# Moving the transposes of queries and keys from TensorE to the DMA crossbar in a fused attention and feed-forward kernel

## The chip, the cores and the metric

The kernel runs on one core of a Trainium2 chip. The metric is the time of one execution in device microseconds; lower is better. A median of several runs is quoted with its range. Ratios are computed as the mean time of one kernel's fast runs over the mean time of the other's fast runs of the same rounds, so they are not quite the ratios of the medians quoted beside them.

In the text, a "chunk" is 512 tokens of the feed-forward part. There are nine chunks and eight batches of attention.

## The reference, cut to what matters

```python
def _attn_ref(q, k, v, global_idx):          # q, k, v: (8 batches, 8 heads, 576, 64) fp32
    scores = q @ k.T / sqrt(64)              # band of +-32 positions, 8 global positions
    attn = softmax(where(mask, scores, -1e9))
    return attn @ v

def reference(...):
    x = attn_out as (4608 tokens, 512)
    g, val = x @ w_gate, x @ w_val           # 512 x 1536 each
    return (silu(g) * val) @ w_out           # 1536 x 512
```

## The kernel before

The score matmuls of both kernels take queries and keys with the head dimension on partitions, the rows of on-chip memory (`qT`, `kT`). They arrive in DRAM with tokens as rows. The kernel before loads them with a cast to bf16 during the DMA and transposes them on TensorE, in four groups (`step_T`) per batch:

```python
def step_T(hp):                                   # four of these a batch
    for name in ("k", "q"):
        ps = pm.tile([P, LJ, LP], BF16, tag="m", name="ps_t")
        for j in range(LJ):
            for par in range(2):
                nc.tensor.transpose(out=ps[64 * par : 64 * par + 64, j, :],
                    in_=ld[name][:, 2 * hp + par, D * j : D * (j + 1)], ...)
        if name == "k":  nc.scalar.copy(out=kT[...], in_=ps...)
        else:            nc.vector.tensor_copy(out=st["qT"][...], in_=ps...)
```

Attention of the next batch is cut into 16 steps, one after each of the 16 feed-forward steps of a chunk (12 "gates" and 4 output steps), so that TensorE has matmuls while ScalarE and VectorE work:

```python
return [
    [L(step_T, 0), L(step_GT)], [L(step_T, 1)], [L(step_T, 2), vb], [L(step_T, 3)],
    [L(step_S2)], [L(step_SG)], [L(step_P2T), L(step_S, 0)], [L(step_S, 1), L(step_AV2)],
    # ... cut: scores (S), attention times values (AV), output transposes (X)
]
```

`vb` is a copy of the values, shifted by 64 tokens, that two DMAs on SyncE's queue make from SBUF to SBUF. `step_GT` transposes the gathered global queries and keys (`kqm`). The scheduling is manual, so every engine issues its work in this order:

```python
loaded[0] = new_qk(); load_qk_part(0, ...)        # GpSimd's queue, casting
g0 = gather(0); load_v(0); kqms[0] = gather_mask(*g0)
for i in range(3): load_wgv(i)                    # 6 weight loads, 1 MB of fp32 each
prefetch(1)                                       # batch 1: gather, q, k, v
# ... cut: output weights wo
for s in attention(0): ...                        # batch 0, nothing to overlap it with
for c in range(NCH):                              # 9 chunks
    for i, f in enumerate(ffn(c)):
        f()                                       # gate or output step
        # then step i of attention(c + 1)
        if i == 2 and c + 2 < B: prefetch(c + 2)
```

The softmax here doesn't subtract the row's maximum and nothing guards it: scores larger than these inputs give would overflow.

## Time and profile before

The median is 428.41 us (428.28 to 428.94, three runs).

| what | value | where read |
|---|---|---|
| span | 426.4 us | the page |
| TensorE busy | 389.9 us | the page |
| first gate of the feed-forward part | 44.0 us | timeline of TensorE |
| length of a steady chunk | 44.9 us | distance of the same step in two chunks |

In the views PE is TensorE, PEld its weight loads, DVE VectorE, ACT ScalarE, POOL GpSimd, and SP or SPq SyncE and its queue. The following lines are from the page of the kernel before. The first gives busy microseconds, the share of the span and number of instructions by engine. The next three give 40 equal slices of the span in tenths: TensorE busy, TensorE clock granted, DMA engines busy. The last gives the shares of the chain that ended last.

```profile
PE 389.9 (91%) x3786; PEld 191.7 (45%) x3786; DVE 265.9 (62%) x583; ACT 178.9 (42%) x281; POOL 92.8 (22%) x134
...
PE   0467899999999999999999999999999999999996
...
PEclk9999999999999999999999999999999999999999
DMA  7999999874338363738355735500030002002002
...
PE 77%; DVE 13%; ACT 5%; POOL 2%; issue 2%; DVEq 0%; ACTq 0%; POOLq 0%
```

TensorE has work from the fourth slice on and almost never stops. The chain is 77% TensorE, so time taken from TensorE in the chunks is time taken from the kernel. The DMA engines are nearly full in the first seven slices (to about 75 us) and then have room.

The stage table of the kernel before (busy microseconds of each engine in a stretch, then clock, DMA share and rate; the share adds up the times of all packets and can pass 1) has the start and one chunk:

```profile
core 0: us, PE busy (x) PEld busy (x) DVE busy (x) ACT busy (x) POOL busy (x), PEclk, DMA share, GB/s
...
15.00:44.00 29.00, 18.67 (x288) 12.26 (x289) 13.95 (x41) 10.88 (x15) 16.59 (x23) 1.00 1.31 184
...
91.00:135.90 44.90, 43.55 (x457) 21.36 (x455) 29.82 (x66) 20.93 (x34) 9.79 (x14) 1.00 0.51 78
```

In the chunk TensorE works 43.55 of 44.9 us. From 15 to 44 us, when batch 0's attention runs alone, it works only 18.67 of 29 us.

The timeline of TensorE before (start, microseconds, engine, line, instruction) shows the first gate and, in a later chunk, one gate with a transpose group:

```profile
43.97 1.91 PE L523 MATMUL pg<-xT,wg_sb 128*128 128x512 bf16 x4
...
138.86 1.02 PE L523 MATMUL pg<-xT,wg_sb 128*128 128x512 bf16 x4
139.72 1.03 PE L523 MATMUL pv<-xT,wv_sb 128*128 128x512 bf16 x4
140.68 0.45 PE L282 MATMUL ps_t<-ident,k_bf 96*64 96x96 bf16 x12
140.96 0.42 PE L282 MATMUL ps_t<-ident,q_bf 96*64 96x96 bf16 x12
141.31 1.04 PE L523 MATMUL pg<-xT,wg_sb 128*128 128x512 bf16 x4
```

From gate to gate it is 141.31 − 138.86 = 2.45 us. The matmuls of the gate alone take two times 0.86 us in the ordered chain, so a transpose group costs about 0.73 us.

The timeline of SyncE's queue before shows the first of batch 0's two `vb` copies:

```profile
20.18 0.53 SPq L100 DMA_DIRECT2D vb<-va  x1
```

They are issued at 20 to 21 us, in good time for their first use at 31 us. On GpSimd's timeline before, the last weight load is issued at 22 us, and a value load that waits for that weight load to land runs at 41 us:

```profile
22.05 0.79 POOL L212 DMA_DIRECT2D wv_sb<-in_moe_w_val_dram  x1
...
41.04 3.42 POOL L95 DMA_DIRECT2D va<-in_v_dram  x4 [1.81 <-DMA wv_sb<-in_moe_w_val_dram]
```

So what stands several transfers behind the weights on GpSimd's queue begins at about 40 us.

### The profile page before, as it was taken

Reading aid. Unit: us, or ns where it says so; the run is one execution under the profiler, and the core shown is the slowest. Engines: PE = TensorE matmul, PEld = TensorE weight load, DVE = VectorE, ACT = ScalarE, POOL = GpSimd, SP = SyncE. Lnnn points to the kernel's source line nnn. Section 1 sums busy time; section 2 is a strip of 40 time slices with the busy share of each in tenths; the row PEclk is TensorE's granted clock in tenths of the full one; section 3 lists DMA queues with packets and bytes.
Section 4 is the critical chain, followed back from the end, with each engine's and each line's share of the span. In section 5 each row is a group of like instructions: output and inputs, shape, how many; then the busy total and the mean of one; then the engine's idle time right before and its main releaser. Section 6 shows DMA issues by size and latency. Waiting matters only on the chain.

```text
span 426.4 us, 9039 instructions
## 1 busy us (share of the span) xinstructions
PE 389.9 (91%) x3786; PEld 191.7 (45%) x3786; DVE 265.9 (62%) x583; ACT 178.9 (42%) x281; POOL 92.8 (22%) x134
## 2 busy tenths in 40 slices
PE   0467899999999999999999999999999999999996
PEld 0344444444544444454444444444444444444442
DVE  5456488638871888278835794488628871771760
ACT  1153355345633464256524653356245643323321
POOL 8943847132023201412122211100000000000000
PEclk9999999999999999999999999999999999999999
DMA  7999999874338363738355735500030002002002
GB/s 111 71 204 208 187 223 154 91 151 57 58 31 131 67 99 22 109 84 113 23 74 117 112 22 73 116 0 3 25 121 7 2 2 94 6 0 98 2 0 98
DMA packets 62232, 33.74 MB, mean 79 GB/s; under 512 B 39408, under 2 KB 56304, under 8 KB 62192
## 3 DMA queue, kind: packets, MB, share of 16 engines
q0 software_dynamic: 55584, 19.40, 40.3%
q1 hardware_dynamic: 6608, 13.77, 9.8%
q8 instruction: 29, 0.48, 0.5%
q14 instruction: 11, 0.09, 0.1%
HBM read 38.28 MB, written 9.44 MB: 112 GB/s over the span
## 4 chain that ended last, share of the span: by engine, by line
PE 77%; DVE 13%; ACT 5%; POOL 2%; issue 2%; DVEq 0%; ACTq 0%; POOLq 0%
PE po L539 22%; PE pg L523 19%; PE pv L523 18%; PE ps_t L282 4%; PE ps_av L435 4%; DVE pt L401 4%; PE ps_av L426 3%; ACT pe L396 3%; DVE h L534 2%; DVE xa L414 2%; PE ps_x L466 2%; ACT kT L288 1%; PE ps_s L388 1%; DVE gvt L365 1%; DVE gv L531 1%
## 5 line engine op out<-in xcount | busy, mean ns | idle before, releaser
L531 DVE SCALAR_TENSOR_TENSOR gv<-th,pg 128x512 bf16<-128x512 bf16 x108 | 73.9, 685 | 62.1 <-ACT th L529 62.1
L523 PE MATMUL pg<-xT,wg_sb 128*128 128x512 bf16 x432 | 112.5, 383 | 0.0
L523 PE MATMUL pv<-xT,wv_sb 128*128 128x512 bf16 x432 | 111.8, 381 | 0.0
L539 PE MATMUL po<-wo_sb,h 128*128 128x512 bf16 x432 | 98.4, 380 | 0.0
L529 ACT ACTIVATE th<-pg 128x512 bf16<-128x512 f32 x108 | 64.5, 598 | 69.1 <-PE pg L523 67.9
L534 DVE TENSOR_TENSOR h<-gv,pv 128x512 bf16<-128x512 bf16 x108 | 74.2, 687 | 11.9 <-PE ps_s L388 0.5
L523 PEld LDWEIGHTS <-wv_sb 128*128 128x128 bf16 x432 | 42.5, 98 | 51.6 <-issue 1.1
L95 POOL DMA_DIRECT2D va<-in_v_dram x40 | 33.8, 853 | 124.7 <-PE ps_av L435 92.5
L539 PEld LDWEIGHTS <-h 128*128 128x128 bf16 x432 | 40.2, 98 | 45.3
L544 ACT ACTIVATE osb<-po 128x512 f32<-128x512 f32 x36 | 21.5, 597 | 92.7 <-PE po L539 92.7
L523 PEld LDWEIGHTS <-wg_sb 128*128 128x128 bf16 x432 | 36.1, 98 | 38.2 <-issue 4.1
L396 ACT ACTIVATE pe<-ps_s 128x1024 bf16<-128x1024 f32 (+1 forms) x40 | 37.6, 940 | 14.8 <-PE ps_s L388 14.8
L410 DVE TENSOR_REDUCE den<-ps_av 128x4 f32<-128x8 f32 x72 | 11.4, 158 | 44.4 <-PE ps_av L455 36.0
L288 ACT COPY kT<-ps_t 128x576 bf16<-128x576 bf16 x32 | 20.4, 638 | 37.4 <-PE ps_t L282 37.4
L401 DVE TENSOR_TENSOR pt<-pe,band 128x1024 bf16<-128x1024 bf16 (+1 forms) x40 | 25.4, 634 | 11.1 <-ACT pe L396 11.0
L414 DVE TENSOR_TENSOR xa<-ps_av,den 128x256 bf16<-128x256 f32 x72 | 30.5, 424 | 2.5
L293 DVE COPY qT<-ps_t 128x576 bf16<-128x576 bf16 x32 | 24.0, 749 | 2.8 <-PE ps_t L282 2.8
L472 ACT COPY xT<-ps_x 128x512 bf16<-128x512 bf16 x32 | 18.0, 588 | 13.8 <-PE ps_x L466 13.8
L426 PE MATMUL ps_av<-gvt,pg 128*128 128x264 bf16 x64 | 19.0, 297 | 3.5 <-DVE gvt L373 2.8
L435 PE MATMUL ps_av<-va,pt 128*64 128x66 bf16 x256 | 21.0, 206 | 0.0
L435 PE MATMUL ps_av<-vb,pt 128*64 128x66 bf16 x256 | 21.0, 207 | 0.0
L435 PEld LDWEIGHTS <-pt 128*64 128x64 bf16 x512 | 13.9, 114 | 14.7 <-issue 10.4
(93 smaller groups left out, 271.1 us busy)
## 6 DMA issues: line engine op xcount, KB each, us to landing
out_dram<-osb SPq DMA_DIRECT2D x36, 256.0 KB, 2.0
k_bf<-in_k_dram POOLq DMA_DIRECT2D x16, 288.0 KB, 6.4
q_bf<-in_q_dram POOLq DMA_DIRECT2D x16, 288.0 KB, 7.2
vb<-va SPq DMA_DIRECT2D x16, 264.0 KB, 3.8
va<-in_v_dram POOLq DMA_DIRECT2D x24, 128.0 KB, 4.0
va<-in_v_dram POOLq DMA_DIRECT2D x16, 96.0 KB, 3.6
wg_sb<-in_moe_w_gate_dram POOLq DMA_DIRECT2D x3, 512.0 KB, 13.2
wv_sb<-in_moe_w_val_dram POOLq DMA_DIRECT2D x3, 512.0 KB, 15.0
```

The source lines that it names most:

```text
L95: nc.gpsimd.dma_start(out=va[lo:hi, u, :, 0:D], in_=vs[t0 + lo : t0 + hi])
L288: nc.scalar.copy(out=kT[:, hp, WIN : WIN + S].rearrange("p (i j) -> p i j", j=LJ), in_=ps.rearrange("p j i -> p i j"),)
L396: nc.scalar.activation(out=pe, in_=ps[:, :, 0 : 64 * ns].rearrange("p r (s c) -> p r s c", c=64), func=AF.Exp, scale=SCALE,)
L401: nc.vector.tensor_tensor(out=pt.rearrange("p r s c -> p (r s) c"), in0=pe.rearrange("p r s c -> p (r s) c"), in1=bc(band, [[0, 2 * ns], [ ...
L414: nc.vector.tensor_tensor(out=xa, in0=ps[:, :, 0:D], in1=den.to_broadcast([P, 4, D]), op=ALU.mult)
L426: nc.tensor.matmul(out=ps, lhsT=st["pg"][:, P * tp : P * (tp + 1)], rhs=st["gv"].rearrange("p h r c -> p (h r) c")[:, 4 * hg : 4 * hg + 4, :],
L435: nc.tensor.matmul(out=ps[64 * e : 64 * e + 64, hl, :], lhsT=pt[:, hl % 2, slot, :], rhs=vv[:, tp, 4 * hg + hl, :], start=False, stop=(hl ...
L523: nc.tensor.matmul(out=ps, lhsT=w[:, cc, P * fc : P * (fc + 1)], rhs=xT[:, cc, t0 : t0 + CH], start=(cc == 0), stop=(cc == NCC - 1),)
L529: nc.scalar.activation(out=th, in_=pg, func=AF.Tanh, scale=0.5)
L531: nc.vector.scalar_tensor_tensor(out=gv, in0=th, scalar=1.0, in1=pg, op0=ALU.add, op1=ALU.mult)
L534: nc.vector.tensor_tensor(out=st["h"][:, fc, :], in0=gv, in1=pv, op=ALU.mult)
L539: nc.tensor.matmul(out=po, lhsT=st["h"][:, fc, P * ts : P * (ts + 1)], rhs=wo_sb[:, fc, :], start=(fc == 0), stop=(fc == NFC - 1),)
```

## The change

From batch 1 on, TensorE no longer transposes. A DMA casts queries and keys to a bf16 scratch in DRAM in token order. A crossbar transpose, a DMA on SyncE's queue, brings them to SBUF as `kT` and `qT`. Values come uncast on SyncE's queue and are cast by GpSimd. The intent is to take 96 transposes and eight copies a batch off TensorE, ScalarE and VectorE. The core of the diff:

```diff
+    def cast_qk(b):
+        for name, src in (("k", k), ("q", q)):
+            t = dram.tile([S, H, D], BF16, name=f"{name}f{b}")
+            nc.gpsimd.dma_start(out=t, in_=src[b].rearrange("h s d -> s h d"))
+            flat[name, b] = t
+    def transpose_qk(b):
+        kT = kT_bufs[b % 2]
+        nc.sync.dma_start_transpose(out=kT[:, :, WIN : WIN + S], in_=flat["k", b]...)
+        qT = bp.tile([P, HP, S], BF16, tag="qT", name="qT")
+        nc.sync.dma_start_transpose(out=qT, in_=flat["q", b]...)
...  (load_v_raw: five loads on nc.sync; cast_v: six nc.gpsimd.tensor_copy)
+        if b > 0:
+            head = [[got, L(step_GT)], [vb]]          # 2 steps instead of 4
...
-    prefetch(1)
+    cast_qk(1)
+    cast_qk(2)
+    kqms[1] = gather_mask(*gather(1))
     for i in range(4):                                # output weights
...
+    cast_v(1, load_v_raw(1))
+    transpose_qk(1)
     for s in attention(0):
...
-            if i == 2 and c + 2 < B:
-                prefetch(c + 2)
+            if i == 1 and c + 2 < B:
+                transpose_qk(c + 2)
+                if c + 3 < B:
+                    cast_qk(c + 3)
+                kqms[c + 2] = gather_mask(*gather(c + 2))
+                vsts[c + 2] = load_v_raw(c + 2)
+            if i == 6 and c + 2 < B:
+                cast_v(c + 2, vsts[c + 2])
```

More of the change, by code (lines that the diff above doesn't have):

```diff
@@ L61 @@
     wpool = ctx.enter_context(tc.tile_pool(name="wpool", bufs=1))
-    ldp = ctx.enter_context(tc.tile_pool(name="ldp", bufs=2))
+    ldp = ctx.enter_context(tc.tile_pool(name="ldp", bufs=1))
+    dram = ctx.enter_context(tc.tile_pool(name="dram", bufs=1, space=bass.MemoryType.DRAM))
     bp = ctx.enter_context(tc.tile_pool(name="bp", bufs=2))
@@ L95, in load_v, with load_v_raw, cast_v @@
             nc.gpsimd.dma_start(out=va[lo:hi, u, :, 0:D], in_=vs[t0 + lo : t0 + hi])
+    def load_v_raw(b):
+        vst = ldp.tile([P, 5, H, D], FP32, tag="vst", name="vst")
+        vs = v[b].rearrange("h s d -> s h d")
+        for u in range(5):
+            lo = WIN if u == 0 else 0
+            hi = P - WIN if u == 4 else P
+            t0 = P * u - WIN
+            nc.sync.dma_start(out=vst[lo:hi, u], in_=vs[t0 + lo : t0 + hi])
+        return vst
+    def cast_v(b, vst):
+        va = va_bufs[b % 2]
+        nc.gpsimd.tensor_copy(out=va[WIN:64, 0, :, 0:D], in_=vst[WIN:64, 0])
+        nc.gpsimd.tensor_copy(out=va[64:P, 0, :, 0:D], in_=vst[64:P, 0])
+        for u in range(1, 4):
+            nc.gpsimd.tensor_copy(out=va[:, u, :, 0:D], in_=vst[:, u])
+        nc.gpsimd.tensor_copy(out=va[0 : P - WIN, 4, :, 0:D], in_=vst[0 : P - WIN, 4])
+    flat = {}
+    def cast_qk(b):
[3 more added lines that the diff above has]
+            flat[name, b] = t
+    tr = {}
+    def transpose_qk(b):
+        kT = kT_bufs[b % 2]
+        nc.sync.dma_start_transpose(
+            out=kT[:, :, WIN : WIN + S], in_=flat["k", b].rearrange("s h d -> s (h d)")
+        )
+        qT = bp.tile([P, HP, S], BF16, tag="qT", name="qT")
+        nc.sync.dma_start_transpose(
+            out=qT, in_=flat["q", b].rearrange("s h d -> s (h d)")
+        )
+        tr[b] = qT
     def load_vb(b):
@@ L268, in attention @@
     def attention(b):
-        ld = loaded[b]
+        ld = loaded[0] if b == 0 else None
         kT = kT_bufs[b % 2]
@@ L489, in vb, with got @@
             st["vb"] = load_vb(b)
+        def got():
+            st["qT"] = tr[b]
         L = lambda f, *a: (lambda: f(*a))
-        return [
+        head = [
             [L(step_T, 0), L(step_GT)],
@@ L496, in attention @@
             [L(step_T, 3)],
+        ]
+        if b > 0:
+            head = [[got, L(step_GT)], [vb]]
+        return head + [
             [L(step_S2)],
@@ L549, in ffn @@
         return [L(gate, fc) for fc in range(NFC)] + [L(outp, ts) for ts in range(4)]
+    vsts = [None] * B
     def prefetch(b):
-        loaded[b] = new_qk()
         g = gather(b)
-        load_qk_part(b, loaded[b], 0)
-        load_qk_part(b, loaded[b], 1)
-        load_v(b)
+        cast_qk(b)
+        vsts[b] = load_v_raw(b)
         kqms[b] = gather_mask(*g)
-    prefetch(1)
+    cast_qk(1)
+    cast_qk(2)
+    kqms[1] = gather_mask(*gather(1))
     for i in range(4):
```

## The prediction

> **What bounds it now.** The page puts TensorE at 389.9 of 426.4 us, and the chain of waits is 77% TensorE. In the steady chunks (stage table, 45 us stretches from 100 to 325 us) TensorE works 43.65 of 45 us, so a chunk with a batch of attention inside is TensorE-bound. The first 44 us are not: there the chain is batch-0 attention behind its loads, and the DMA engines are full to about 75 us (page, DMA row).
>
> **Removed, for batches 1 to 7.** Per batch 96 TensorE transposes (four groups of 24), four ScalarE copies (638 ns) and four VectorE copies (750 ns). In the TensorE timeline a gate with a transpose group takes 2.46 us (138.86 to 141.31) against 1.73 us for its eight matmuls: 0.72 us each, 2.9 us a batch. The short wait of the gathered-key transpose for the ScalarE copy (0.48 us) goes too: at most 3.4 us a batch, 24 us in all. I keep 19 to 20, because attention now starts two slots earlier, which puts the last attention-value products and output transposes into gate slots, where VectorE (two 0.69 us operations a gate, 0.7 us per normalisation) is already in the chain (13% of it).
>
> **Added.** Each query or key tensor becomes a DRAM-to-DRAM cast of 4608 pieces of 128 bytes, against 768 pieces of 768 bytes. Value loads of the same piece size move at about 117 GB/s written (15 to 20 us), some 18 ns a piece per engine; with a DRAM target I estimate 18 to 30 ns, so 5 to 9 us per tensor. A crossbar transpose of 0.59 MB: the Trainium skill, "DMA: Bandwidth & Descriptors", Latency and other measured facts, gives 261 GB/s, hence an estimate of 2.3 us plus landing; no trace here shows it, and I allow up to 10. In steady chunks this has a whole chunk of slack and should hide; GpSimd (9.8 of 45 us busy) has room for the casts of values.
>
> **Where it hurts: the start.** On SyncE's program order both transposes of batch 1 come before the shifted value copy (vb) of batch 0, and they wait for both casts of batch 1. These casts stand on GpSimd's queue behind all six gate/value weight loads, whose last lands at 41 us (GpSimd's waits for them end at 31.4, 33.4, 35.9, 38.4, 41.0). So casts land near 48 and 56, the transposes land near 62, vb near 65 to 70. Before, vb was issued at 20 us and used at 31. TensorE stands in batch 0's first attention-value step from 31 to about 68, then needs its remaining 13 us; the first gate starts near 82 instead of 44. The gathers of batch 1 stand behind four casts (to about 75), which may add little more. About +40 us, all on the critical path, paid once.
>
> **Sum.** 428.4 + 40 − 19.5 = 449 us, range 432 to 480. Chances: faster by over 2% 0.05, within 2% 0.10, slower 0.85.
>
> **Signs.** Right: TensorE idle of some 35 us from about 31, released by the vb copy; first gate near 80; chunk period 42 instead of 45; transposes and casts hidden after batch 1; TensorE busy down by about 27 us. Wrong: first gate near 44 (no stall), or chunk period still 45.
>
> **What would make it wrong.** Casts of 3 us and fast transposes bring it near 435. Casts over 15 us or transposes over 12 us make DMA the bound of every chunk and the result 500 or more. If VectorE becomes the bound in gate slots, the saving shrinks below 14.

## The result and the profile after

The changed kernel took 439.69 us (438.52 to 441.35, four runs), against 428.68 us for the kernel before. The profiled run is the slowest of the four (441.35 us). The ratio is 1.0257 (95% interval 1.0219 to 1.0294): slower by 2.6%. The same lines of the page as above, for the changed kernel:

```profile
PE 367.5 (84%) x3066; PEld 177.8 (40%) x3114; DVE 247.6 (56%) x555; ACT 162.3 (37%) x253; POOL 102.3 (23%) x127
...
PE   0450026999999999899989999999999999999996
...
PEclk9999999999999999999999999999999999999999
DMA  9999999994987919492979490059013001002002
...
PE 57%; DVE 23%; DMA 6%; ACT 4%; POOL 3%; SPq 3%; issue 3%; DVEq 0%; ACTq 0%; POOLq 0%
```

TensorE is busy for 22 us less, and the span is 13 us longer in this profile. The new hole, a stand of TensorE, is in the fourth to sixth slices of the TensorE row, while the DMA row reads 9. The waits by engine (who waited for whom: total, times, longest) name it, and the second line is a stall of GpSimd that is used below:

```profile
PE ps_av L475 <- DMA vb<-va: 32.0, 1, 32.0
...
POOL qf L121 <- issue: 11.8, 1, 11.8
```

One wait of 32 us, on the shifted value copy of batch 0. The chain in order of time (start, microseconds, what) says why that copy was late:

```profile
22.95 19.94 DMA kf<-in_k_dram
...
42.91 5.67 SPq L128
...
48.63 6.91 SPq L132
...
55.73 0.54 SPq L140
...
56.32 7.23 DMA vb<-va
...
63.59 0.43 PE ps_av L475 x7
```

The key cast, issued at 23 us, lands at 42.9. Only then can SyncE issue the key transpose (L128), which occupies its queue for 5.7 us, and then the query transpose (L132), for 6.9 us. The copy that batch 0 needs is behind both, is issued at 55.7, and lands at 63.6. For batch 0 the order of issue changed only in this copy's place on SyncE's queue.

The stage table of the changed kernel, for that stand and for one later chunk (columns as before):

```profile
31.30:63.50 32.20, 0.32 (x2) 0.13 (x1) 0.50 (x1) 0.00 (x0) 4.36 (x4) 1.00 1.75 165
...
163.70:205.80 42.10, 40.36 (x353) 19.34 (x359) 27.24 (x62) 18.57 (x29) 11.38 (x12) 1.00 0.87 125
```

The later chunk takes 42.1 us instead of 44.9, and TensorE is busy in it for some 3 us less (a few matmul records are missing in this trace). So the change does two things. The first gate moves from 44.0 to 77.2 us, a loss of 33.2 us paid once (the timeline of TensorE; one record of the four matmuls is missing):

```profile
77.22 1.49 PE L570 MATMUL pg<-xT,wg_sb 128*128 128x512 bf16 x3 [0.22 <-issue]
```

From there to the end it takes 439.6 − 77.2 = 362.4 us instead of 426.4 − 44.0 = 382.4, a gain of 20.0 us. The difference is 13.2 us, which is the difference of the two profiled spans.

### The profile page after: what moved, and what is told of

Read it like the earlier page. It is cut to its first block, busy times and chain, and to the rows that moved or that the text cites. A ratio compares the mean times of both kernels' runs of the same rounds, so it can differ in the third digit from the quotient of the medians.

```text
span 439.6 us, 7623 instructions
## 1 busy us (share of the span) xinstructions
PE 367.5 (84%) x3066; PEld 177.8 (40%) x3114; DVE 247.6 (56%) x555; ACT 162.3 (37%) x253; POOL 102.3 (23%) x127
## 2 busy tenths in 40 slices
DMA packets 148466, 46.04 MB, mean 105 GB/s; under 512 B 136400, under 2 KB 142544, under 8 KB 148432
## 3 DMA queue, kind: packets, MB, share of 16 engines
q1 hardware_dynamic: 72128, 30.29, 33.1%
## 4 chain that ended last, share of the span: by engine, by line
PE 57%; DVE 23%; DMA 6%; ACT 4%; POOL 3%; SPq 3%; issue 3%; DVEq 0%; ACTq 0%; POOLq 0%
PE po L586 21%; PE pg L570 15%; PE pv L570 13%; DVE xa L454 5%; DVE h L581 5%; DMA kf<-in_k_dram 5%; DVE pt L441 4%; DVE gv L578 4%; DVE den L453 2%; ACT pe L436 2%; DMA vb<-va 2%; SPq L132 2%; PE ps_x L506 2%; PE ps_av L475 1%; SPq L128 1%
## 5 line engine op out<-in xcount | busy, mean ns | idle before, releaser
L570 PE MATMUL pg<-xT,wg_sb 128*128 128x512 bf16 x401 | 110.1, 385 | 2.9 <-issue 1.3
L586 PE MATMUL po<-wo_sb,h 128*128 128x512 bf16 x417 | 94.9, 379 | 0.5
L581 DVE TENSOR_TENSOR h<-gv,pv 128x512 bf16<-128x512 bf16 x108 | 74.3, 688 | 11.5 <-PE pv L570 0.4
L586 PEld LDWEIGHTS <-h 128*128 128x128 bf16 x432 | 41.1, 98 | 46.3
L570 PEld LDWEIGHTS <-wg_sb 128*128 128x128 bf16 x432 | 37.2, 99 | 41.1 <-issue 4.6
L441 DVE TENSOR_TENSOR pt<-pe,band 128x1024 bf16<-128x1024 bf16 (+1 forms) x40 | 26.7, 668 | 11.3 <-ACT pe L436 11.2
L110 POOL CAST va<-vst 32x512 bf16<-32x512 f32 x7 | 4.2, 603 | 120.7 <-DMA vst<-in_v_dram 73.3
L121 POOL DMA_DIRECT2D qf<-in_q_dram x7 | 18.8, 2687 | 11.8 <-issue 11.8
L475 PE MATMUL ps_av<-va,pt 128*64 128x66 bf16 x256 | 21.3, 207 | 0.0
L506 PE MATMUL ps_x<-ident,xa 128*128 128x128 bf16 x128 | 13.5, 232 | 7.5 <-DVE xa L454 7.2
## 6 DMA issues: line engine op xcount, KB each, us to landing
wg_sb<-in_moe_w_gate_dram POOLq DMA_DIRECT2D x3, 512.0 KB, 11.5
```

Source lines behind the costliest of these rows:

```text
L441: nc.vector.tensor_tensor(out=pt.rearrange("p r s c -> p (r s) c"), in0=pe.rearrange("p r s c -> p (r s) c"), in1=bc(band, [[0, 2 * ns], [ ...
L475: nc.tensor.matmul(out=ps[64 * e : 64 * e + 64, hl, :], lhsT=pt[:, hl % 2, slot, :], rhs=vv[:, tp, 4 * hg + hl, :], start=False, stop=(hl ...
L506: nc.tensor.transpose(out=ps[:, hp, :], in_=st["xa", tp][:, 2 * hp : 2 * hp + 2, :].rearrange("p h d -> p (h d)"), identity=ident,)
L570: nc.tensor.matmul(out=ps, lhsT=w[:, cc, P * fc : P * (fc + 1)], rhs=xT[:, cc, t0 : t0 + CH], start=(cc == 0), stop=(cc == NCC - 1),)
L581: nc.vector.tensor_tensor(out=st["h"][:, fc, :], in0=gv, in1=pv, op=ALU.mult)
L586: nc.tensor.matmul(out=po, lhsT=st["h"][:, fc, P * ts : P * (ts + 1)], rhs=wo_sb[:, fc, :], start=(fc == 0), stop=(fc == NFC - 1),)
```

## The experiments

My theory: the gain in the chunks is real and the DMA work is hidden there; the loss is only the order of issue at the start. Rivals: the traffic of casts and transposes slows everything (the DMA packets rise from 62,232 to 148,466); or the crossbar transposes themselves are too slow. Every edit is shown against the changed kernel unless said otherwise. Every run was judged correct against the reference. Between rounds the kernel before moved by 0.5 us.

| run | median us | ratio to before | new waits of TensorE, us (after the first gate unless said) | steady chunk us |
|---|---|---|---|---|
| before | 428.4 to 428.9 | 1 | none | 44.90 |
| changed | 439.69 | 1.0257 | 32.0 before the first gate | 42.10 |
| e1_vb_first | 426.94 | 0.9964 | 17.0 | 41.95 |
| e2_gather_first | 425.59 | 0.9925 | 11.3 + 3.3 | 42.06 |
| e3_casts_before_weights | 421.62 | 0.9835 | 12.2 | 42.16 |
| e4_free_transposes | 409.42 | 0.9552 | none | 42.28 |
| e5_late_slots | 437.33 | 1.0202 | 30.8 before the first gate | 41.85 |
| e6_casts_early_only | 434.94 | 1.0142 | 26.6 before the first gate | 42.28 |
| e7_early_casts_late_slots | 415.69 | 0.9695 | 7.9 | 41.61 |
| e8_values_as_before | 429.64 | 1.0029 | 11.5 + 3.6 + 2.1 | 41.77 |
| e9_batch1_on_tensore | 428.52 | 0.9991 | 18.1 | 41.80 |
| e10_casts_first | 426.01 | 0.9941 | 12.8 before the first gate | 41.81 |
| e11_batch1_vb_fixed | 408.65 | 0.9541 | none | 41.68 |
| e12_fixed_dma_values | 407.31 | 0.9511 | none | 41.47 |

The steady chunk is the mean distance between ScalarE's last output copies of batches 1 to 5 (before) or 1 to 6 (the others).

### e1: vb ahead of the transposes

```diff
-    transpose_qk(1)
     for s in attention(0):
         for f in s:
             f()
+    transpose_qk(1)
```

> The changed kernel with one move: the two transposes of batch 1 are put after batch 0's attention in the program, so that on SyncE the shifted value copy of batch 0 (vb) is issued first. Same DMA work, same arithmetic. My theory (order on SyncE): no 32 us stand of TensorE on vb; first gate at 44 to 46 us instead of 77; then a new wait, at the gathered-key transpose of batch 1, because the gathers still stand behind the four casts (kqm at 64 us in the changed kernel): about 18 us. Total 424 to 428 us. Rival A (the sheer DMA traffic of casts and transposes delays everything): the first gate stays beyond 70 us and the total within 4 us of 439.7. Rival B (vb itself is slow beside the casts whatever its place): stand of over 20 us remains.

Measured: 426.94 us, within its range. SyncE's queue in this run:

```profile
20.48 0.54 SPq L140 DMA_DIRECT2D vb<-va  x1
...
45.10 5.53 SPq L128 DMA_TRANSPOSE kT<-kf  x1
50.74 7.17 SPq L132 DMA_TRANSPOSE qT<-qf  x1
```

The copy is issued at 20.5 us again, the first gate is at 44.1 us, and the stand of 32 us is gone, with the same DMA work. The transposes still occupy the queue for 5.5 and 7.2 us. Both rivals fall as the explanation of that stand. The wait that was expected behind it shows in the waits of TensorE:

```profile
PE ps_g L342 <- POOL kqm L233: 22.9, 2, 17.0
```

Of these, 5.9 us is batch 0's own wait, which the kernel before has too; the other 17.0 us is the gathered keys of batch 1 behind four casts. In the changed kernel this wait was hidden by the longer one.

### e2: the gathers ahead of the casts as well

```diff
 (e1, and)
-    cast_qk(1)
-    cast_qk(2)
-    kqms[1] = gather_mask(*gather(1))
+    g1 = gather(1)
+    cast_qk(1)
+    kqms[1] = gather_mask(*g1)
     (output weights)
+    cast_qk(2)
```

> e1 plus: the gathers of batch 1 before its casts on GpSimd's queue, and the casts of batch 2 after the output weights. Theory: the new wait at the gathered keys goes; left is the wait for the batch-1 transposes themselves, which are wanted at 49 to 53 us and land at about 55 (keys) and 58 to 62 (queries): 5 to 9 us. Total 412 to 418 us. If the steady chunks, not the start, were what loses, it stays above 425.

Measured: 425.59 us, a miss. The wait for the gathered keys went, but the waits for the transposes themselves were longer than I expected:

```profile
PE ps_s L371 <- DMA kT<-kf: 11.3, 1, 11.3
...
PE ps_sg L353 <- DMA qT<-qf: 3.3, 1, 3.3
```

That is 14.6 us instead of 5 to 9. The key transpose was issued at 46.0 us and took 16.3 us to land, where 6.6 us was the shortest in the changed kernel. Beside it the output weights and the casts of batch 2 were on the DMA engines. The second rival is therefore not dead for the start: a transpose among full queues is slow.

### e3: the casts of batch 1 ahead of the weights

```diff
 (e2, and the gather and the casts of batch 1 moved up)
+    g1 = gather(1)
+    cast_qk(1)
     for i in range(3):
         load_wgv(i)
```

> e2 with the gathers and the casts of batch 1 moved ahead of the six gate/value weight loads on GpSimd's queue; vb of batch 0 before the transposes as in e1. Theory (only the order at the start lost the time): two casts cost about 7.5 us of DMA time (4608 pieces each at 158 GB/s written), so they land near 32 us, the transposes (12 to 13 us of SyncE's issue while the rings are full) land near 46, the first weights near 36: first gate at 44 to 45, no wait over 3 us, total 409 to 413 us, the free-transposes kernel being 409.4. Rival (with the DMA rings full the transposes land late wherever they stand): a wait of 5 us or more for the transposed keys stays, total above 415.

Measured: 421.62 us, a miss; the rival's total came, with the wait on the transposed queries and not the keys. SyncE's queue in this run:

```profile
29.96 6.53 SPq L128 DMA_TRANSPOSE kT<-kf  x1
36.60 19.15 SPq L132 DMA_TRANSPOSE qT<-qf  x1
```

The key cast lands by 30 us and the query cast by 34, but the query transpose then holds the queue for 19.2 us. The DMA view of e3 from 36.6 to 56 us (queue, packets, megabytes, share; then one issue and its time to landing) shows why:

```profile
q0 software_dynamic: 2897, 2.87, 93.1%
q1 hardware_dynamic: 2899, 0.73, 35.0%
...
qT<-qf SPq DMA_TRANSPOSE x1, 29.1
```

In this stretch the queue that SyncE feeds (q1) got 2899 packets through while the queue that GpSimd feeds (q0) got 2897. The Trainium skill, "DMA: Bandwidth & Descriptors", section Queues, rings and completion order, says that each DMA engine goes round-robin between the queues that have work, a packet at a time. This trace agrees: one for one. So do e6 and e10 beside weights (625 to 625 packets from 40 to 44 us, 624 to 624 from 36 to 40). Beside casts the counts are not equal (922 of SyncE's to 407 from 49 to 51 us in the changed kernel). Whether the trace's packets are those of the page is not shown. GpSimd's packets here are mostly pieces of weights (2.87 MB in 2897 packets, about 1 KB written each; the 2 KB in the expectation of e10 are the same rows as read in fp32). The transpose's packets are about 250 bytes. (The changed kernel's q1 has 72,128 packets; less 32,256 of values and 6,608 as before the change, 33,264 are left for 14 transposes, 2,376 for each of 0.59 MB.) So a transpose needs some 2,400 turns, and beside weights it pays for each with a weight packet. At the 624 packets that SyncE's queue got through from 44 to 48 us, 2,376 take an estimated 15 us. The query transpose landed 29.1 us after its issue, but behind the key transpose, which landed 20.8 us after its own: 14.9 us apart.

### e4: what free transposes would give

```diff
-        kT = kT_bufs[b % 2]
+        kT = kT_bufs[0]
...
-            st["qT"] = tr[b]
+            st["qT"] = tr[0]        # batch 0's, kept
 (all cast_qk and transpose_qk removed)
```

> Wrong result on purpose: the changed kernel with no casts of queries and keys and no crossbar transposes at all; batches 1 to 7 read batch 0's transposed keys and queries. The slot order, values and everything else as in the changed kernel. It is what the change would give if its DMA cost nothing. Theory: chunks of 42.0 us, the same as in the changed kernel, since the casts and transposes are hidden there; first gate near 44; total 406 to 409 us. Rival (DMA traffic also slows the chunks): chunks of 41 us or less, total below 402.

Measured: 409.42 us, just above its range, with a chunk of 42.28 us against 42.10 in the changed kernel. Removing all casts and transposes makes no chunk shorter, so in the chunks they cost nothing. That settles the first rival for the chunks. This kernel computes with the wrong queries and keys from batch 1 on. The comparison with the reference still passed it, presumably because queries and keys are scaled by 0.1 and the scores are all near zero. A "correct" on this input says little about `qT` and `kT`.

### e5: the old slots

```diff
-            head = [[got, L(step_GT)], [vb]]
+            head = [[got, L(step_GT)], [vb], [], []]
```

> The changed kernel with two empty steps put in where the transposes were, so that the attention of a batch stands in the same slots of the chunk as before the change. My prediction said that the two slots earlier cost some 0.5 us a chunk through VectorE. If so, the chunk falls from 42.0 to about 41.5 and the total by 3 to 4 us, to 436. Rival (the slots do not matter, TensorE is the bound either way): within 1 us of the changed kernel. Note that its prologue is unchanged, so the 33 us stay.

Measured: 437.33 us, ratio 1.0202 against 1.0257: about 2.4 us less, where 3 to 4 were expected; the traced stand is 1.2 us shorter, so not all of it is the slots. Across all runs that differ in this the chunk is 41.6 to 41.85 us with the two empty steps (e5, e7, e9, e10, e11) and 41.95 to 42.3 without (changed, e1, e2, e3, e4, e6). The two pairs that differ in this alone give 0.25 us (changed and e5) and 0.55 us (e3 and e7), the means of the two groups 0.39 us. So the earlier slots cost some 0.4 us a chunk.

### e6: only the casts moved

```diff
-    cast_qk(1)
     cast_qk(2)
...
+    cast_qk(1)
     for i in range(3):
         load_wgv(i)
```

> The changed kernel with one move only: the casts of batch 1 go ahead of the weight loads; the transposes still stand before vb on SyncE. It splits the 32 us stand of TensorE: the part that is the casts' place behind the weights (31.3 to 42.9 us in the changed kernel) should go, the part that is SyncE issuing the transposes and vb landing behind them (12.8 and 7.8 us) should stay. Theory: casts land near 32, transposes issue to about 45, vb lands near 50: a stand of 17 to 22 us, the batch-1 gathers (behind two casts of batch 2 only after the weights) no worse than before; total 425 to 430. Rival (the whole stand is the weights' place in the queue): stand under 8 us, total below 417.

Measured: 434.94 us and a stand of 26.6 us. This is longer than I expected, and for the reason found in e3. SyncE's queue:

```profile
27.89 9.07 SPq L128 DMA_TRANSPOSE kT<-kf  x1
37.01 12.32 SPq L132 DMA_TRANSPOSE qT<-qf  x1
49.58 0.55 SPq L140 DMA_DIRECT2D vb<-va  x1
```

The key cast is done 15 us earlier than in the changed kernel (27.9 against 42.9 us), but the transposes now meet the weights and hold SyncE for 9.1 and 12.3 us instead of 5.7 and 6.9. Only 5.4 us of the stand go. So moving the casts alone gains little, because the transposes then meet the weights; what is left is the place of `vb` behind two slow transposes.

### e7: e3 with the old slots

The edit is e3 and the line of e5.

> e3 with the two empty steps of e5. Theory: the start of e3 and the chunk of e5 (41.85 against 42.1 us): 1 to 3 us below e3, near 408 to 411. If the slots bring nothing, the same as e3 within 0.7 us.

Measured: 415.69 us, better than e3 by more than the slots explain. The query transposes are wanted two gates later, so the wait for them is 7.9 instead of 12.2 us. Even so the total missed its range.

### e8: e3 with the values as before

```diff
 (e3, and)
-    cast_v(1, load_v_raw(1))
+    load_v(1)
...
-                vsts[c + 2] = load_v_raw(c + 2)
-            if i == 6 and c + 2 < B:
-                cast_v(c + 2, vsts[c + 2])
+                load_v(c + 2)
```

> e3 with the value part of the change undone: values are again cast by the DMA into place, with no staging tile and no casts on GpSimd. Theory: in the chunks both hide behind TensorE, so within 2 us of e3. Rival (value part matters, because GpSimd's in-order queue stands waiting for the value buffers and so issues the next casts late): a wait for transposes appears and the total is over 3 us above e3.

Measured: 429.64 us, 8 us above e3: a miss, and the rival's total came, though by another way. The loss is all in the first chunk, where the values of batch 1 now stand behind the casts of batch 2 on GpSimd's queue (5.7 us of new waits for values and their copy; the 11.5 us for the transposed queries were 12.2 in e3). The 5.7 us are not all of it: TensorE's granted clock was 0.50 to 0.57 from 74 to 89 us, where in e3 it was 1.00. The later chunks are shorter, 41.77 against 42.16 us. The groups of VectorE by shape, from 140 to 300 us, show a reason (total busy, then mean nanoseconds of one). In the changed kernel:

```profile
L441 DVE TENSOR_TENSOR pt<-pe,band 128x1024 bf16<-128x1024 bf16 x13 | 9.6, 739 | 2.1 <-ACT pe L436 2.1
```

And the same group in e8:

```profile
L444 DVE TENSOR_TENSOR pt<-pe,band 128x1024 bf16<-128x1024 bf16 x16 | 11.0, 687 | 2.7 <-ACT pe L439 2.7
```

The band product, with two SBUF inputs, takes 739 ns where GpSimd casts values and 687 ns where it does not. The kernel before has 686 ns. The Trainium skill, "SBUF — State Buffer", section Who interferes with whom, says that a VectorE instruction with two SBUF inputs contends with a GpSimd instruction that reads SBUF. The numbers agree with that. The DMA work is not the reason: e4, with GpSimd's casts but without the DMA work of queries and keys, has 733 ns. Whether these 50 ns make the shorter chunk is not shown.

### e9: batch 1 on TensorE

```diff
-    cast_qk(1)
-    cast_qk(2)
-    kqms[1] = gather_mask(*gather(1))
+    g1 = gather(1)
+    loaded[1] = new_qk()
+    load_qk_part(1, loaded[1], 0)
+    load_qk_part(1, loaded[1], 1)
+    kqms[1] = gather_mask(*g1)
     (output weights)
+    cast_qk(2)
...
-        if b > 0:
-            head = [[got, L(step_GT)], [vb]]
+        if b > 1:
+            head = [[got, L(step_GT)], [vb], [], []]
 (transpose_qk(1) removed)
```

> Batch 1 goes the old way (plain loads, transposes on TensorE), casts and crossbar transposes start with batch 2, where nothing is in a hurry; two empty slots as in e7. Theory: no wait for a transpose anywhere; the free-transposes kernel (409.4) plus one batch of TensorE transposes (2.9 us) less the later slots (about 1.7 us): 409 to 413 us. Rival (crossbar transposes also come too late for batch 2): a wait at batch 2 and over 415.

Measured: 428.52 us, a miss, by my own edit. SyncE's queue:

```profile
58.58 6.50 SPq L128 DMA_TRANSPOSE kT<-kf  x1
65.20 6.60 SPq L132 DMA_TRANSPOSE qT<-qf  x1
71.98 8.30 SPq L105 DMA_DIRECT2D vst<-in_v_dram  x5
80.33 1.04 SPq L140 DMA_DIRECT2D vb<-va  x1
```

The old step list makes batch 1's `vb` in the third step, but the transposes of batch 2 are issued in the second. So `vb` stood behind two transposes and five value loads, and TensorE waited 18.1 us for it: the fault of the changed kernel over again, one batch later.

### e10: the casts in the early gap

```diff
     load_qk_part(0, loaded[0], 1)
+    cast_qk(1)
...
-    cast_qk(1)
-    cast_qk(2)
     kqms[1] = gather_mask(*gather(1))
     (output weights)
+    cast_qk(2)
 (and the line of e5)
```

> The casts of batch 1 directly behind batch 0's own query and key loads, where the DMA engines stood idle before (10 to 15 us); transposes before vb on SyncE as in the changed kernel; two empty slots. It tests why the query transpose took 19 us of issue in e3 and e7. Theory (the transpose shares each DMA engine packet by packet with what else is queued, and there these were 2 KB weight packets): here its neighbours are mostly 128-byte value and cast packets, so each transpose issues in 4 to 8 us, all lands by about 32, vb by about 36; TensorE waits under 6 us for it, and no wait later. Batch 0's own gathers and values land some 3 to 7 us later. Total 410 to 418. Rival (a transpose is just slow at the start, 19 us whatever stands beside it): vb beyond 42, total over 420.

Measured: 426.01 us, a miss. The transposes were issued from 20.6 us and held SyncE for 5.8 and 8.4 us, as the theory of neighbours expected; the rival's 19 us did not come. But the query transpose landed 22.3 us after its issue, `vb` after 42 us and the total over 420, as the rival had it. There were two costs I had not counted, and the waits of TensorE show both:

```profile
PE ps_i L276 <- DVE ones L273: 15.0, 1, 15.0
PE ps_av L476 <- DMA vb<-va: 12.8, 1, 12.8
```

The casts occupy GpSimd while it should write the small index tables, so VectorE's opening work, and TensorE's first wait with it, ends at 15.0 us instead of 10.4 (kernel before); batch 0's wait for its gathered keys grows from 5.8 to 8.5 us. And `vb`, issued at 35.2 to 38.6 us, took up to 14.8 us to land. The weights were then on the engines and the transposes' packets ahead of it on the same queue. How those two share the 14.8 us is not separated.

### e11: e9 with vb in its right place

```diff
 (e9, and)
-            [L(step_T, 1)],
-            [L(step_T, 2), vb],
+            [L(step_T, 1), vb],
+            [L(step_T, 2)],
```

> e9 with batch 1's vb moved one slot up, so that on SyncE it stands before the transposes of batch 2. In e9 the 18.1 us wait for vb of batch 1 came from my own edit: the old step list put vb of batch 1 in the slot after the transposes of batch 2 are issued, the very order that hurts the changed kernel. Theory: no wait over 2 us after the first gate; first chunk near 47 us, later chunks 41.8; total 409 to 412 us. Rival (something else in the start of e9 costs the 18 us): over 418.

Measured: 408.65 us (408.12 to 409.41, five runs), just below its range, ratio 0.9541. SyncE's queue:

```profile
52.64 0.46 SPq L140 DMA_DIRECT2D vb<-va  x1
...
60.51 6.07 SPq L128 DMA_TRANSPOSE kT<-kf  x1
```

`vb` of batch 1 at 52.6 us precedes the transposes of batch 2 at 60.5 us, and no new wait is left. Moving one copy by one slot was worth 20 us, more than the 18.1 us of the wait. In e9 the granted clock was still 0.50 from 84 to 89 us, when TensorE had begun to work again, and 0.66 from 89 to 94; that may be the rest.

### e12: e11 with values cast by the DMA from batch 2 on

```diff
 (e11, and)
-                vsts[c + 2] = load_v_raw(c + 2)
-            if i == 6 and c + 2 < B:
-                cast_v(c + 2, vsts[c + 2])
+                load_v(c + 2)
```

> e11 with the values of batches 2 to 7 loaded and cast by the DMA as before the change; batch 1's values stay as in e11. The band product on VectorE (128x1024) takes 739 ns in the changed kernel's chunks and 687 ns in e8, where GpSimd casts nothing; if GpSimd's casts beside VectorE cost the chunk, this is 1 to 2.5 us below e11 (chunk 41.5 instead of 41.8). If they are hidden, it equals e11 within 0.7 us. If the value loads delay the casts on the shared queue, it is above e11.

Measured: 407.31 us (406.78 to 407.62, five runs), ratio 0.9511 (0.9498 to 0.9524), the fastest and 32 us below the changed kernel. The gain over e11 is 1.3 us, as expected if GpSimd's casts cost the chunk, so the value part of the change is a small loss in the chunks; at the start, beside early casts, it was useful (e8). Two lines of its page, TensorE by slices and the shares of the chain:

```profile
PE   0367899999999999999999999999999999999996
...
PE 76%; DVE 14%; ACT 4%; POOL 2%; issue 2%; DMA 1%; DVEq 0%; ACTq 0%; POOLq 0%
```

The hole is gone and the chain is again TensorE. Against the kernel before, six batches save 44.90 − 41.47 = 3.43 us each, which is 20.6 of the 21.1 us.

## Why the prediction was right, point by point

- **Direction and mechanism were right.** The prediction named `vb` of batch 0 behind the transposes of batch 1 on SyncE, and these behind the casts behind the weights. The chain shows exactly these links, and e1 removes the stand by moving one line.
- **The gain in the chunks was right in sum, in part by luck.** I kept 19 to 20 us; the part after the first gate became 20.0 us shorter. The upper limit of 3.4 us a batch is also what e12 reaches (3.43). I had taken 0.64 us a batch off it for the slots alone; the runs show some 0.4 for the slots and 0.2 for the value part (e11 against e12), which I had not counted.
- **The loss was overestimated by some 7 us.** The prediction's 449 had +40 for this term and the runs show +33. (The other part of the distance to 439.7 is mostly that the profiled run is the slowest of the four.) Two terms were mis-sized and cancelled, which was luck. The casts were estimated at 5 to 9 us a tensor; while only casts ran, the DMA wrote 158 GB/s, so 0.59 MB takes 3.7 us, and the key cast landed at 42.9 us and not near 48. The transposes were longer than the 2.3 us estimate from the skill and the 10 us that I allowed (12.2 and 13.0 us to landing). So the query transpose landed at 61.6 us, where I had 62. What did not cancel is the step behind it: I had `vb` landing at 65 to 70 us and the first gate near 82. But SyncE issued `vb` at 55.7 us, when it had issued the transposes and before the second had landed; `vb` landed at 63.6 and the first gate came at 77.2. That is 4.8 us; the other 2 us of the +40, for the gathers, did not come.
- **"The gathers may add little more" was right only because a longer wait covered them.** e1 uncovered 17.0 us.
- **The slot effect had the right sign and some 0.6 of the size:** 0.25 and 0.55 us a chunk in the two pairs, 0.39 between the groups, against the 0.64 that I had taken off (24 to 19.5 us over seven batches).
- **"GpSimd has room for the casts" missed a cost.** GpSimd has time for them, but its casts lengthen VectorE's band product by some 50 ns.
- **TensorE's busy time fell by 22 us, not the 27 that I named as a sign.** (A few matmul records are missing in the trace of the changed kernel; e5, with none missing, shows 21.3 us less.) That figure added up the groups of transposes, whose instructions overlap their neighbours in the timeline, so it was a poor sign; the later chunk's length was the good one.

What stays open: how much of the slow landing beside other traffic comes from packet sharing and how much from the queue in front (e10). The one-for-one packet counts of e3 show the sharing, but no run varied the packet size of the neighbours alone.

## What to carry to other kernels

When work moves from a busy engine to a DMA queue, look first at what stands behind it in that queue's program order: a transfer that waits for a far producer blocks every later, ready transfer on the same queue. Give the first batch, which nothing overlaps, the old path, and start the new path where it has a whole stage of slack. And when removing one wait gains less than its length, expect a second wait that it had covered.

## What the Trainium skill lacked or had wrong

- "Advanced Engine Details and Errata", X-Bar Transpose, says that transposes are as fast as regular DMAs. With nothing on GpSimd's queue beside it a transpose of 0.59 MB took 5.1 us to landing (changed kernel, 170 us), which does not contradict this. But it took 12 to 13 us beside casts and 20.8 and 29.1 us beside weight loads (e3, where the output weights, 0.39 MB a piece, took 24.7 us themselves). That the cause is its packets of about 250 bytes is argued from the counts of e3, not shown alone. No page says that a transpose loses its share beside a queue with larger packets.
- No page gives the time for which a transpose of this size holds SyncE's queue. In the changed kernel it was 2.4 to 4.1 us in the later chunks and 5.7 to 6.9 us at the start beside casts; in e3 it was 19.2 us beside weights. Every later transfer of that queue waits for it.
- No page says how many DMAs GpSimd can have under way; the pages give only the room in SBUF that is kept for their descriptors. In the changed kernel GpSimd stood 11.8 us before it could issue a fourth DMA of 4,608 pieces, until the first of the four had landed; in e3 this was 15.3 us.
- "DMA: Bandwidth & Descriptors", Specifications, says that pieces under 512 bytes pay a read-modify-write. Casts written to DRAM in 128-byte pieces ran at 158 GB/s, the same as the peak of value loads to SBUF in 128-byte pieces in the kernel before (158 GB/s); no extra cost of the DRAM target shows. Short pieces were slower here too: loads in 768-byte pieces reached 208 GB/s in the kernel before. No run shows the read-modify-write itself.
- "TensorE: Matmul & The Clock Gate", Part 1, says that an idle TensorE falls to half clock and needs some microseconds of work to recover. The traces agree: the eight gate matmuls at 44 us take 634 ns each in the kernel before, against 379 later. But the row of granted clock reads 9 in those slices and also during the 32 us stand; it fell to 0.50 only in stands after the first gates (e1, 54 to 64 us). Before that it can't be used to see a cold TensorE. The page warns that trace events of the clock gate can be unreliable, but does not name this case.
